# The last twelve chunks of a second expert weight in two column halves, eleven token tiles likewise

## The chip, the cores and the metric

The kernel runs on one core of a Trainium2 chip. Its time is the device time of one execution in microseconds (us); the program before has a median of 178.85 us over four runs (178.42 to 179.23). Engines are named as in the profile: PE is the matrix engine (PEld its weight load), DVE the vector engine, ACT the scalar engine, POOL is GpSimd, SP the sync engine. POOL and SP issue DMAs here: all loads of q, k, v and the expert weights go from POOL's queue (q0, with a cast from float32 to bfloat16 on the way), the stores of the result from SP's queue (q1).

## The reference, cut to what matters

Attention with a sliding window (heads 0 to 3) or a dilated one (heads 4 to 7), and behind it a soft mixture of 8 experts with 4 slots each.

```python
scores = q @ k.T / sqrt(64); masked to rel in [0, 32) or to every 4th of [0, 128)
x = softmax(scores) @ v              # 8 x 8 heads x 576 x 64 -> 4608 tokens x 512
logits = x @ phi                     # 4608 x 32 slots
d = exp(logits), normalised over the tokens;  slot_input = d.T @ x      # 32 x 512
for e in range(8):
    slot_out[e] = relu(slot_input[e] @ w1[e]) @ w2[e]     # 512 -> 1024 -> 512, 4 slots
c = exp(logits), normalised over the slots
out = c @ slot_out                   # 4608 x 512, float32
```

The result is 9.44 MB. The two weights, w1 and w2, are 16.8 MB each in float32.

## The kernel before

**Attention.** Eight units (a pair of batches and four heads each) are transposed, multiplied, masked and normalised. This part runs to about 131 us, and nothing in it is changed. It leaves `expT`, the exponentials of the logits by slot and token, and sums for the slot inputs.

**Experts.** w1 is held in seven parts of `WD` and one of `stg`. The hidden layer is in `hT` (16 chunks of 128 rows, slots as columns) at 141.5 us. The second layer accumulates in one pair of PSUM banks, `sp_`: column half 0 (output columns 0 to 255) in the first bank, half 1 in the second. w2 comes in groups of two experts; each partition holds 16 rows ("chunks" c of 512 columns, 32 KB of contiguous float32 in memory). The list `PARTS` (L893) gives the order in which PE consumes them (L901): p3a (group 3, chunks 0 to 7), p0, p1, p2, p3b (chunks 8 to 13) and p3c (chunks 14 and 15). `wload` (L444) loads each with one DMA, except p0, which goes out in 13 pieces (`skewed`, L460): 112 rows in four DMAs, 16 rows in small groups, and small reads into `scr` between them[...]. Six more tiny reads (`steps`, L815) go out between p2 and p3b.

**Output.** A row sum (`rsum`, L928) gives each token's normaliser, `rtok`. When the second layer is complete, DVE (L939) and ACT (L943) copy the two halves of `sp_` to `so_sb`. The 36 groups of 128 tokens are put into six token tiles of 1, 2, 3, 5, 9 and 16 groups (`TILES`, L887); the kernel calls a group j of such a tile. PE multiplies a group with `so_sb` (L973, 512 columns; the first group in two halves, L971), ACT and DVE by turns scale it into a staging area in SBUF (L985, L986), and when a tile is complete SP stores it with one DMA (L994). In memory a tile of n groups is n x 2 KB contiguous per partition.

**Order.** Every operation is entered with `op`, with a key and an assumed cost. `schedule` plays the program through with these costs and writes down, per engine, the order of the instructions; among operations that could start within 0.1 us of each other the smaller key goes first. POOL and SP keep the order in which their operations are entered. The semaphores follow from the data. A few plain matmuls with no use for the result are put in so that PE does not idle: a number in the stretches that the plan leaves empty (L1003), and seven (`WARM`) of them behind p2 (L917, key 1003.9, ahead of p3b with 1004).

Of the kernel before, what the change touches and what calls it, by code (L numbers as in the profile page):

```python
# [317 lines left out]
def bass_dilated_sliding_attn__then__soft_moe_slots_kernel(  # L318
# [14 lines left out]
    def sb(name, shape, dt=BF16):  # L333
# [3 lines left out]
    TURNS = ((15, None, 0), (6, 39, 8), (2, None, 0), (2, 7, 8), (6, None, 0), (6, 87, 8), (2, None, 0),  # L337
             (2, 23, 8), (7, None, 0))
    STEPS = (3, 2, 11, 4, 2, 10)
# [28 lines left out]
    scr = sb("scr", [16, len(TURNS), 2, 32])  # L368
# [25 lines left out]
    def bank(t):  # L394
        return ps[:, t.phys[0], :]
# [48 lines left out]
    def wload(name):  # L444
# [3 lines left out]
        if name[:2] == "w1":  # L448
            src = moe_w1[int(name[2:])].rearrange("(p c) f -> p c f", c=4)
            dst = ap.rearrange("p (c f) -> p c f", c=4)  # L450
        else:
            g = int(name[1])
            c = {"": slice(0, 16), "a": slice(0, 8), "b": slice(8, 14), "c": slice(14, 16)}[name[2:]]
            src = moe_w2[2 * g:2 * g + 2].rearrange("e (p c) f -> (e p) c f", c=16)[:, c, :]
            dst = ap.rearrange("p (c f) -> p c f", f=512)
        if name == "p0":
# [3 lines left out]
            def skewed(g):  # L460
                res = [g.dma_start(dst[r:128:n], src[r:128:n])
                       for r, n in ((0, 4), (1, 4), (2, 4), (3, 8))]
                for i, (n, r, step) in enumerate(TURNS):
                    if r is None:
                        res.append(g.dma_start(scr[0:n, i], src[0:n, :, 0:32]))
                    else:
                        e = r + step * (n - 1) + 1
                        res.append(g.dma_start(dst[r:e:step], src[r:e:step]))
                return res
            op("pool", skewed, after=b.prev, a=[b], cost=0.6 * (4 + len(TURNS)), sem=sem, nbytes=512 * 8192,  # L470
               nd=288, nq=4 + len(TURNS))
            return
        cut = [slice(None)]
        op("pool", lambda g: [g.dma_start(dst[:, x], src[:, x]) for x in cut], after=b.prev, a=[b],
           cost=0.6 * len(cut), sem=sem, nbytes=512 * ap.shape[1], nd=128 * len(cut), nq=len(cut))
# [4 lines left out]
    home(stg[:, 2, 4096:8192], [b_stg[2]], "p3a")  # L480
# [4 lines left out]
    home(TTf[:, 8192:11264], b_TT, "p3b")  # L485
    home(TTf[:, 11264:12288], b_TT, "p3c")
# [326 lines left out]
    s_scr = DmaSem(nc, "s_scr")  # L813

    def steps(g):  # L815
        res, lo = [], 8704
        for i, n in enumerate(STEPS):
            w = 8 * (i + 1)
            res.append(g.dma_start(stg[0:n, 0, lo:lo + w], moe_w1[0, 0:n, 0:w]))  # L819
            lo += w  # L820
        return res
    op("pool", steps, after=HOME["p0"][1].prev, cost=0.6 * len(STEPS), sem=s_scr, nbytes=16384,
       nd=8 * len(STEPS), nq=len(STEPS))
    wload("p3b")
    wload("p3c")
# [61 lines left out]
    for n in (1, 2, 3, 5, 9, 16):  # L887
        TILES.append((128 * sum(x[1] for x in TILES), n))
# [4 lines left out]
    PARTS = [("p3a", 3, 0, 8), ("p0", 0, 0, 16), ("p1", 1, 0, 16), ("p2", 2, 0, 16),  # L893
             ("p3b", 3, 8, 14), ("p3c", 3, 14, 16)]
    for k_, (name, g, c0, c1) in enumerate(PARTS):
        wv = HOME[name][0].rearrange("p (c f) -> p c f", f=512)
        for h_ in range(2):
            def pe(t, k_=k_, name=name, g=g, c0=c0, c1=c1, h_=h_, wv=wv):
                for c in range(c0, c1):
# [3 lines left out]
                                  wv[:, c - c0 + (1 if name == "p0" and c > 7 else 0), 256 * h_:256 * h_ + 256],  # L903
                                  start=(k_ == 0 and c < c0 + 4), stop=(k_ > 3 and c >= 12))
# [4 lines left out]
                       key=K1 + 2 + 0.5 * k_ + 0.1 * h_)  # L909
# [26 lines left out]
    for h_ in range(2):  # L936
        sl = slice(256 * h_, 256 * h_ + 256)
        if h_ == 0:
            op("dve", lambda vv, sl=sl: vv.tensor_scalar(so_sb[:, sl], pair(sp_)[:, 0, 0:256],  # L939
                                                         rcs[:, 0:1], None, op0=AluOp.mult),  # L940
               r=[b_sp[0], b_rcs], w=[b_so[0]], cost=0.35, key=K1 + 20)
        else:
            op("act", lambda ac, sl=sl: ac.activation(so_sb[:, sl], pair(sp_)[:, 1, 0:256],  # L943
                                                      ACTF.Copy, scale=rcs[:, 0:1]),
               r=[b_sp[1], b_rcs], w=[b_so[1]], cost=0.4, key=K1 + 20)

    for o_ in P.ops[-2:]:
# [4 lines left out]
    w17f, p0f = [HOME[x][0].bitcast(F32) for x in ("w17", "p0")]  # L952
    wdh = [f"w1{e}" for e in range(7)]
    STAGE = [(w17f[:, 0:512], ["w17"]), (w17f[:, 512:1536], ["w17"]),
             (WDf[:, 12800:14336], wdh), (p0f[:, 0:2560], ["p0"]),
             (WDf[:, 8192:12800], wdh), (WDf[:, 0:8192], wdh)]
    nev = 0
    for o, (t0, n) in enumerate(TILES):
        ost = STAGE[o][0].rearrange("p (j f) -> p j f", j=n)
        ob = Buf()  # L960
        for h_ in STAGE[o][1]:
            ob.prev = ob.prev + HOME[h_][1].ready + HOME[h_][1].reads
        for j0 in range(0, n, 2):
            po = tile(psum, 2)
            split = n == 1
            kk = K1 + 30 + o + 0.1 * j0
            b_po = [Buf(), Buf()]
            for j in range(2 if split else min(2, n - j0)):
                def pe(t, o=o, po=po, j0=j0, j=j, split=split):
                    if split:  # L970
                        return t.matmul(pair(po)[:, j, 0:256], tok[o][0],  # L971
                                        so_sb[:, 256 * j:256 * j + 256], start=True, stop=True)
                    return t.matmul(pair(po)[:, j, :], tok[o][j0 + j], so_sb[:],  # L973
                                    start=True, stop=True)
                p0 = op("pe", pe, r=(b_so[j:j + 1] if split else b_so) + b_expT, a=[po],
                        w=[b_po[j]], alloc=[po] if j == 0 else [], after=[p0] if j else [],
                        cost=0.12 if split else 0.22, key=kk + 0.01 * j)
                col = rcol[o] + (0 if split else j0 + j)

                def ev(en, po=po, ost=ost, j=j, j0=j0, split=split, col=col):  # L980
                    d_ = ost[:, 0, 256 * j:256 * j + 256] if split else ost[:, j0 + j, :]
                    s_ = pair(po)[:, j, 0:256 if split else 512]
                    sc_ = rtok[:, col:col + 1]
                    if en is nc.scalar:
                        return en.activation(d_, s_, ACTF.Copy, scale=sc_)  # L985
                    return en.tensor_scalar(d_, s_, sc_, None, op0=AluOp.mult)  # L986
                o_ = op(("dve", "act")[(j + nev) % 2], ev, r=[b_po[j], b_rtok], a=[ob], after=ob.prev,
                        cost=0.35 if split else 0.6, key=kk)
                o_.touch.append(po)
                po.left += 1  # L990
            nev += 0 if split else n - j0 == 1
        so = DmaSem(nc, f"s_out{o}")
        s_out.append(so)
        op("sp", lambda e, t0=t0, n=n, ost=ost: [e.dma_start(  # L994
# [62 lines left out]
```

## Time and profile before

| what | value |
|---|---|
| median of four runs | 178.85 us |
| the profiled execution's own time | 178.61 us |
| its span, first to last instruction | 176.9 us |
| granted TensorE clock, mean | 0.93 |
| busy: PE, DVE, ACT, POOL | 134.5, 113.0, 96.1, 44.1 us |
| read from memory, written to it | 61.94 MB, 9.44 MB |
| q0 (loads with cast), q1 (stores) | 30.95 MB and 9.50 MB moved |

The bytes of q0 are counted where they land, in bfloat16; twice as many are read. An engine's busy time is a sum over stages with different limits; the row of digits "DMA" on the profile's page shows in which tenth of each of 40 slices (4.4 us each) the 16 DMA engines were busy, and "PEclk" which clock PE was granted. In answers by stretch of time, "DMA share" can lie above 1.00, because the records of two packets on one DMA engine overlap a little.

### The profile page before, as it was taken

Reading aid. Unit: us, or ns where it says so; the run is one execution under the profiler, and the core shown is the slowest. Engines: PE = TensorE matmul, PEld = TensorE weight load, DVE = VectorE, ACT = ScalarE, POOL = GpSimd, SP = SyncE. Lnnn points to the kernel's source line nnn. Section 1 sums busy time; section 2 is a strip of 40 time slices with the busy share of each in tenths; the row PEclk is TensorE's granted clock in tenths of the full one; section 3 lists DMA queues with packets and bytes.
Section 4 is the critical chain, followed back from the end, with each engine's and each line's share of the span. In section 5 each row is a group of like instructions: output and inputs, shape, how many; then the busy total and the mean of one; then the engine's idle time right before and its main releaser. Section 6 shows DMA issues by size and latency. Waiting matters only on the chain.

```text
span 176.9 us, 5795 instructions
## 1 busy us (share of the span) xinstructions
PE 134.5 (76%) x2604; PEld 104.7 (59%) x2609; DVE 113.0 (64%) x256; ACT 96.1 (54%) x141; POOL 44.1 (25%) x87
## 2 busy tenths in 40 slices
PE   0019799779999896899968899986999997798000
PEld 0019698667897685697757778864656693342000
DVE  6850297936987995987974799899440200699300
ACT  2005779645985883977864788786311000699000
POOL 7990705202502501700200780107200000000000
PEclk9999999956999999999996999999999999789755
DMA  5999999999999999999999999999999998299995
GB/s 82 200 221 212 208 221 214 214 213 215 220 208 212 217 214 208 220 220 210 214 218 216 209 213 220 219 209 210 214 233 226 193 203 169 110 424 452 437 474 237
DMA packets 6504, 40.81 MB, mean 231 GB/s; under 512 B 2256, under 2 KB 2256, under 8 KB 2896
## 3 DMA queue, kind: packets, MB, share of 16 engines
q0 software_dynamic: 5088, 30.95, 84.7%
q1 hardware_dynamic: 1392, 9.50, 12.9%
q8 instruction: 20, 0.33, 0.7%
q14 instruction: 4, 0.03, 0.0%
HBM read 61.94 MB, written 9.44 MB: 404 GB/s over the span
## 4 chain that ended last, share of the span: by engine, by line
PE 45%; DMA 20%; DVE 11%; ACT 8%; issue 5%; POOL 3%; DVEq 0%; POOLq 0%
DMA TT<-in_moe_w_dram 15%; PE ps L576 11%; PE ps L571 7%; PE ps L668 5%; PE ps L614 5%; PE ps L639 5%; DMA stg<-in_k_dram 5%; DVE WD L986 4%; ACT PT L621 4%; PE ps L723 4%; PE ps L696 3%; ACT TT L596 3%; PE ps L973 2%; PE ps L754 2%; POOL stg L819 2%
## 5 line engine op out<-in xcount | busy, mean ns | idle before, releaser
L621 ACT ACTIVATE PT<-ps 128x768 bf16<-128x768 f32 x48 | 37.1, 816 | 10.5 <-PE ps L614 10.2
L596 ACT ACTIVATE TT<-ps 128x864 f32<-128x864 f32 x32 | 28.6, 896 | 21.7 <-PE ps L576 18.8
L679 DVE TENSOR_TENSOR XB<-ps,RV 96x768 bf16<-96x768 f32 x32 | 30.4, 951 | 0.9
L576 PE MATMUL ps<-ident,stg 96*64 96x96 bf16 x576 | 19.9, 241 | 14.5 <-DMA stg<-in_k_dram 12.5
L576 PEld LDWEIGHTS ps<-ident,stg 96*64 96x64 bf16 x576 | 17.8, 136 | 15.8 <-DMA stg<-in_k_dram 12.5
L644 DVE COPY VN<-ps 128x768 bf16<-128x768 bf16 x32 | 17.0, 542 | 11.5 <-PE ps L639 11.5
L614 PE MATMUL ps<-TT 64*128 64x96 bf16 x384 | 16.6, 214 | 7.3 <-issue 4.3
L668 PE MATMUL ps<-VN,PT 128*128 128x65 bf16 x384 | 18.5, 198 | 1.8 <-DVE XB L679 0.6
L428 POOL DMA_DIRECT2D stg<-in_q_dram x16 | 8.8, 551 | 43.1 <-PE ps L576 26.6
L668 PEld LDWEIGHTS ps<-VN,PT 128*128 128x128 bf16 x384 | 15.3, 101 | 3.2 <-DVE VN L644 0.9
L614 PEld LDWEIGHTS ps<-TT 64*128 64x128 bf16 x384 | 10.4, 99 | 11.4 <-issue 4.6
L639 PE MATMUL ps<-ident,TT 128*128 128x128 bf16 x192 | 16.1, 226 | 0.4 <-ACT PT L621 0.3
L709 ACT ACTIVATE XT<-ps 128x576 bf16<-128x576 bf16 x22 | 13.7, 652 | 2.6 <-PE ps L696 2.6
L571 PE MATMUL ps<-ident,stg 96*128 96x96 bf16 x288 | 14.7, 206 | 0.0
L696 PE MATMUL ps<-ident,XB 96*128 96x96 bf16 x192 | 13.2, 213 | 1.6 <-DVE XB L679 1.1
L629 DVE TENSOR_TENSOR PT<-PT,mask_p 128x768 bf16<-128x768 bf16 x24 | 12.8, 548 | 1.7 <-ACT PT L621 1.3
L571 PEld LDWEIGHTS ps<-ident,stg 96*128 96x128 bf16 x288 | 13.2, 98 | 1.0 <-issue 0.2
L629 DVE TENSOR_TENSOR PT<-PT,mask_d 128x768 bf16<-128x768 bf16 x24 | 13.0, 546 | 0.8 <-ACT PT L621 0.5
L639 PEld LDWEIGHTS ps<-ident,TT 128*128 128x128 bf16 x192 | 11.5, 100 | 2.3 <-ACT PT L621 0.5
L696 PEld LDWEIGHTS ps<-ident,XB 96*128 96x128 bf16 x192 | 9.9, 102 | 3.4 <-DVE XB L679 1.6
L973 PE MATMUL ps<-so_sb,expT 128*128 128x512 bf16 x34 | 10.8, 449 | 0.3 <-issue 0.2
L708 DVE COPY XT<-ps 128x576 bf16<-128x576 bf16 x10 | 5.8, 576 | 7.3 <-PE ps L696 7.1
(87 smaller groups left out, 183.5 us busy)
## 6 DMA issues: line engine op xcount, KB each, us to landing
WD<-in_moe_w_dram POOLq DMA_DIRECT2D x7, 1024.0 KB, 29.4
stg<-in_q_dram POOLq DMA_DIRECT2D x16, 288.0 KB, 19.4
stg<-in_v_dram POOLq DMA_DIRECT2D x16, 288.0 KB, 20.1
stg<-in_k_dram POOLq DMA_DIRECT2D x16, 288.0 KB, 21.0
out_dram<-WD SPq DMA_DIRECT2D x1, 4096.0 KB, 11.4
out_dram<-WD SPq DMA_DIRECT2D x1, 2304.0 KB, 7.0
stg<-in_moe_w_dram POOLq DMA_DIRECT2D x2, 1024.0 KB, 29.8
stg<-in_moe_w_dram POOLq DMA_DIRECT2D x1, 2048.0 KB, 24.2
```

What stands on the lines that cost most here:

```text
L571: i_ = t.transpose(bankb2(pt, a)[:, 96 * kk:96 * kk + 96], two[:, j // 2, c, :], ident[0:96, 0:96])
L576: i_ = t.transpose(bankb2(pt, a)[64 * hx:64 * hx + 64, 96 * kk:96 * kk + 96], src[:, hx, c, :], ident[0:96, 0:96])
L596: return ac.activation(d, sv, ACTF.Copy)
L614: i_ = t.matmul(pair(sc)[:, hx, QB * x:QB * x + QB], win(u, 1, h01, blk_, bpar)[64 * hx:64 * hx + 64], win(u, 0, h01, blk_, bpar)[64 * hx: ...
L621: op("act", lambda ac: ac.activation(sbt(pt)[:, 0:768].rearrange("p (x n) -> p x n", x=2), pair(sc)[:, :, 0:384], ACTF.Exp, scale=SCALE), ...
L629: return dv.tensor_tensor(p_, p_, m.unsqueeze(1).to_broadcast([128, 2, 384]), AluOp.mult)
L639: i_ = t.transpose(bankb(pv)[:, 128 * m:128 * m + 128], win(u, 2, h01, m, bpar), ident[:, :])
L644: op("dve", lambda dv: dv.tensor_copy(sbt(vn)[:, :, :, 0:64], bankb(pv)[:, 0:768].rearrange("p (m x d) -> p m x d", m=6, x=2)), r=[pv], w= ...
L668: i_ = t.matmul(pair(po)[:, bk, 65 * po_:65 * po_ + 65], sbt(pts[i])[:, o_:o_ + 128], sbt(vn)[:, m, half, 0:65], start=True, stop=True)
L679: op("dve", lambda dv: dv.tensor_tensor(sbt(xb)[:].rearrange("p m (x h d) -> p h x m d", x=2, h=2)[:, h01], pv()[:, :, :, 0:64], sbt(rv)[: ...
L696: i_ = t.transpose(bankb(px)[:, QB * m:QB * m + QB], sbt(xb)[:, m, 128 * x:128 * x + 128], ident[0:QB, 0:QB])
L973: return t.matmul(pair(po)[:, j, :], tok[o][j0 + j], so_sb[:], start=True, stop=True)
```

## The change

The last group of w2 is cut anew. p3a shrinks from eight chunks to four. The other twelve are loaded in two column halves: p3b and p3c hold chunks 4 to 13 and 14 to 15 for output columns 0 to 255, p3d and p3e the same chunks for columns 256 to 511. A run of such a load is 1 KB of float32 in memory and 512 bytes in SBUF. The four are entered behind p2 in this order, p3b now into a free part of `stg`. PE's work on p3d and p3e has a key 28 higher, behind the first token tiles of half 0.

The token tiles become 1, 2, 3, 5, 4, 8 and 13 groups. The first four (eleven groups) are computed and stored twice, first columns 0 to 255, then columns 256 to 511; the other three as before. In a halved tile two groups share a PSUM bank, and DVE empties such a bank with one `tensor_tensor` (the normaliser broadcast over 256 columns), ACT with two activations; the plan chooses between the two engines. A halved tile's store has runs of 1 KB in memory. There are 11 stores in place of six, all from SP's queue (`POOLS` is False). The tiles' staging areas move.

The second half of `so_sb` may be copied by DVE or ACT. The six tiny reads between p2 and p3b are removed, and p0's 13 pieces come in another order, with other small groups for its last 16 rows.

```diff
@@ -334,9 +334,11 @@
         return A(nc.sbuf_tensor(name, shape, dt))
 
     WARM = 7
-    TURNS = ((15, None, 0), (6, 39, 8), (2, None, 0), (2, 7, 8), (6, None, 0), (6, 87, 8), (2, None, 0),
-             (2, 23, 8), (7, None, 0))
-    STEPS = (3, 2, 11, 4, 2, 10)
+    TURNS = ((32, 0, 4), (32, 1, 4), (32, 2, 4), (16, 3, 8), (15, None, 0), (6, 39, 8), (2, None, 0),
+             (2, 87, 8), (6, None, 0), (4, 103, 8), (2, 7, 8), (2, None, 0), (2, 23, 8))
+    W2 = {"p3a": (3, 0, 4, 0, 512), "p0": (0, 0, 16, 0, 512), "p1": (1, 0, 16, 0, 512),
+          "p2": (2, 0, 16, 0, 512), "p3b": (3, 4, 14, 0, 256), "p3c": (3, 14, 16, 0, 256),
+          "p3d": (3, 4, 14, 256, 512), "p3e": (3, 14, 16, 256, 512)}
     NPT, NVN, NXB, NXT, NET = 6, 5, 5, 4, 2
     WD = sb("WD", [128, 7, 4096])
     stg = sb("stg", [128, 3, 9216])
...
@@ -449,41 +451,42 @@
             src = moe_w1[int(name[2:])].rearrange("(p c) f -> p c f", c=4)
             dst = ap.rearrange("p (c f) -> p c f", c=4)
         else:
-            g = int(name[1])
-            c = {"": slice(0, 16), "a": slice(0, 8), "b": slice(8, 14), "c": slice(14, 16)}[name[2:]]
-            src = moe_w2[2 * g:2 * g + 2].rearrange("e (p c) f -> (e p) c f", c=16)[:, c, :]
-            dst = ap.rearrange("p (c f) -> p c f", f=512)
+            g, c0, c1, f0, f1 = W2[name]
+            src = moe_w2[2 * g:2 * g + 2].rearrange("e (p c) f -> (e p) c f", c=16)[:, c0:c1, f0:f1]
+            dst = ap.rearrange("p (c f) -> p c f", f=f1 - f0)
         if name == "p0":
             src = src.rearrange("p (x c) f -> p x (c f)", x=2)
             dst = ap.rearrange("p (x y) -> p x y", x=2)[:, :, 0:4096]
 
             def skewed(g):
-                res = [g.dma_start(dst[r:128:n], src[r:128:n])
-                       for r, n in ((0, 4), (1, 4), (2, 4), (3, 8))]
+                res = []
                 for i, (n, r, step) in enumerate(TURNS):
                     if r is None:
-                        res.append(g.dma_start(scr[0:n, i], src[0:n, :, 0:32]))
+                        res.append(g.dma_start(scr[0:n, i], src[0:n, :, 0:8]))
                     else:
                         e = r + step * (n - 1) + 1
                         res.append(g.dma_start(dst[r:e:step], src[r:e:step]))
                 return res
-            op("pool", skewed, after=b.prev, a=[b], cost=0.6 * (4 + len(TURNS)), sem=sem, nbytes=512 * 8192,
-               nd=288, nq=4 + len(TURNS))
+            op("pool", skewed, after=b.prev, a=[b], cost=0.6 * (len(TURNS)), sem=sem, nbytes=512 * 8192,
+               nd=288, nq=len(TURNS))
             return
-        cut = [slice(None)]
-        op("pool", lambda g: [g.dma_start(dst[:, x], src[:, x]) for x in cut], after=b.prev, a=[b],
-           cost=0.6 * len(cut), sem=sem, nbytes=512 * ap.shape[1], nd=128 * len(cut), nq=len(cut))
+        op("pool", lambda g: [g.dma_start(dst, src)], after=b.prev, a=[b], cost=0.6, sem=sem,
+           nbytes=512 * ap.shape[1], nd=128)
 
     for e in range(7):
         home(WD[:, e, :], [], f"w1{e}")
     home(stg[:, 2, 0:4096], [b_stg[2]], "w17")
-    home(stg[:, 2, 4096:8192], [b_stg[2]], "p3a")
+    home(stg[:, 2, 4096:6144], [b_stg[2]], "p3a")
+    home(stg[:, 2, 6144:8704], [b_stg[2]], "p3b")
     home(stg[:, 0, :], [b_stg[0]], "p0")
     home(stg[:, 1, 0:8192], [b_stg[1]], "p1")
     TTf = TT[:].rearrange("p a x -> p (a x)")
     home(TTf[:, 0:8192], b_TT, "p2")
-    home(TTf[:, 8192:11264], b_TT, "p3b")
-    home(TTf[:, 11264:12288], b_TT, "p3c")
+    lo = 8192
+    for n_ in ("p3c", "p3d", "p3e"):
+        hi = lo + 256 * (W2[n_][2] - W2[n_][1])
+        home(TTf[:, lo:hi], b_TT, n_)
+        lo = hi
 
     load_unit(0)
     op("sp", lambda e: [e.dma_start(phi_st[:], moe_phi.rearrange("(c p) s -> p c s", p=128))],
@@ -810,19 +813,8 @@
             for bpar in range(2):
                 st_L(u - 1 + bpar, u)
     wload("p2")
-    s_scr = DmaSem(nc, "s_scr")
-
-    def steps(g):
-        res, lo = [], 8704
-        for i, n in enumerate(STEPS):
-            w = 8 * (i + 1)
-            res.append(g.dma_start(stg[0:n, 0, lo:lo + w], moe_w1[0, 0:n, 0:w]))
-            lo += w
-        return res
-    op("pool", steps, after=HOME["p0"][1].prev, cost=0.6 * len(STEPS), sem=s_scr, nbytes=16384,
-       nd=8 * len(STEPS), nq=len(STEPS))
-    wload("p3b")
-    wload("p3c")
+    for n_ in ("p3b", "p3c", "p3d", "p3e"):
+        wload(n_)
 
     K1 = 1000.0
     op("dve", lambda vv: vv.tensor_reduce(rcs[:], csum[:], mybir.AxisListType.X, AluOp.add),
@@ -884,29 +876,30 @@
         op("act" if p_ == 0 else "dve", ev, r=[ht], w=[b_hT[p_]], cost=0.35, key=K1)
 
     TILES = []
-    for n in (1, 2, 3, 5, 9, 16):
+    NSPLIT = 4
+    POOLS = False
+    for n in (1, 2, 3, 5, 4, 8, 13):
         TILES.append((128 * sum(x[1] for x in TILES), n))
     tok = [[expT[:, t0 + j:t0 + j + n * 127 + 1:n] for j in range(n)] for t0, n in TILES]
     rcol = [sum(n for _, n in TILES[:i]) for i in range(len(TILES))]
     sp_ = tile(psum, 2)
     b_sp = [Buf(), Buf()]
-    PARTS = [("p3a", 3, 0, 8), ("p0", 0, 0, 16), ("p1", 1, 0, 16), ("p2", 2, 0, 16),
-             ("p3b", 3, 8, 14), ("p3c", 3, 14, 16)]
-    for k_, (name, g, c0, c1) in enumerate(PARTS):
-        wv = HOME[name][0].rearrange("p (c f) -> p c f", f=512)
-        for h_ in range(2):
-            def pe(t, k_=k_, name=name, g=g, c0=c0, c1=c1, h_=h_, wv=wv):
+    for k_, name in enumerate(W2):
+        g, c0, c1, f0, f1 = W2[name]
+        wv = HOME[name][0].rearrange("p (c f) -> p c f", f=f1 - f0)
+        for h_ in range(f0 // 256, f1 // 256):
+            def pe(t, k_=k_, name=name, g=g, c0=c0, c1=c1, h_=h_, wv=wv, f0=f0):
                 for c in range(c0, c1):
                     j = c % 4
                     i_ = t.matmul(pair(sp_)[32 * j:32 * j + 32, h_, 0:256],
                                   hT[:, c, 24 * g:24 * g + 32],
-                                  wv[:, c - c0 + (1 if name == "p0" and c > 7 else 0), 256 * h_:256 * h_ + 256],
-                                  start=(k_ == 0 and c < c0 + 4), stop=(k_ > 3 and c >= 12))
+                                  wv[:, c - c0 + (name == "p0" and c > 7), 256 * h_ - f0:256 * h_ - f0 + 256],
+                                  start=(k_ == 0 and c < 4), stop=(k_ > 3 and c >= 12))
                 return i_
             last_ = op("pe", pe, r=b_hT + [HOME[name][1]], alloc=[sp_] if k_ == h_ == 0 else [],
                        a=[sp_, b_sp[h_]], cost=0.13 * (c1 - c0) / 4, mode="c",
                        ni=2 * (c1 - c0),
-                       key=K1 + 2 + 0.5 * k_ + 0.1 * h_)
+                       key=K1 + 2 + 0.5 * k_ + 0.1 * h_ + (28 if k_ > 5 else 0))
             if k_ == 2:
                 mid = last_
         if k_ == 3:
@@ -935,65 +928,83 @@
 
     for h_ in range(2):
         sl = slice(256 * h_, 256 * h_ + 256)
...
     for o_ in P.ops[-2:]:
         o_.touch.append(sp_)
         sp_.left += 1
 
...
     nev = 0
-    for o, (t0, n) in enumerate(TILES):
+    for o, h_ in [(o, h_) for h_ in range(2) for o in range(NSPLIT)] + [(o, None) for o in range(NSPLIT, 7)]:
+        t0, n = TILES[o]
         ost = STAGE[o][0].rearrange("p (j f) -> p j f", j=n)
+        sl = slice(0, 512) if h_ is None else slice(256 * h_, 256 * h_ + 256)
         ob = Buf()
-        for h_ in STAGE[o][1]:
-            ob.prev = ob.prev + HOME[h_][1].ready + HOME[h_][1].reads
+        for x in STAGE[o][1]:
+            ob.prev = ob.prev + HOME[x][1].ready + HOME[x][1].reads
+        k1 = K1 + 30 + o + 10 * (2 if h_ is None else h_)
+        w = sl.stop - sl.start
         for j0 in range(0, n, 2):
-            po = tile(psum, 2)
-            split = n == 1
-            kk = K1 + 30 + o + 0.1 * j0
+            po = tile(psum, w // 256)
+            kk = k1 + 0.1 * j0
             b_po = [Buf(), Buf()]
-            for j in range(2 if split else min(2, n - j0)):
-                def pe(t, o=o, po=po, j0=j0, j=j, split=split):
-                    if split:
-                        return t.matmul(pair(po)[:, j, 0:256], tok[o][0],
-                                        so_sb[:, 256 * j:256 * j + 256], start=True, stop=True)
-                    return t.matmul(pair(po)[:, j, :], tok[o][j0 + j], so_sb[:],
-                                    start=True, stop=True)
-                p0 = op("pe", pe, r=(b_so[j:j + 1] if split else b_so) + b_expT, a=[po],
+
+            def slot(j, po=po, w=w):
+                if w == 512:
+                    return pair(po)[:, j, :]
+                return bank(po)[:, w * j:w * j + w]
+            m = min(2, n - j0)
+            for js in [range(m)] if w == 256 else [(j,) for j in range(m)]:
+                def pe(t, o=o, slot=slot, j0=j0, js=js, sl=sl):
+                    for j in js:
+                        i_ = t.matmul(slot(j), tok[o][j0 + j], so_sb[:, sl], start=True, stop=True,
+                                      skip_group_check=True)
+                    return i_
+                j = js[0]
+                p0 = op("pe", pe, r=(b_so if h_ is None else b_so[h_:h_ + 1]) + b_expT, a=[po],
                         w=[b_po[j]], alloc=[po] if j == 0 else [], after=[p0] if j else [],
-                        cost=0.12 if split else 0.22, key=kk + 0.01 * j)
-                col = rcol[o] + (0 if split else j0 + j)
-
-                def ev(en, po=po, ost=ost, j=j, j0=j0, split=split, col=col):
-                    d_ = ost[:, 0, 256 * j:256 * j + 256] if split else ost[:, j0 + j, :]
-                    s_ = pair(po)[:, j, 0:256 if split else 512]
-                    sc_ = rtok[:, col:col + 1]
-                    if en is nc.scalar:
-                        return en.activation(d_, s_, ACTF.Copy, scale=sc_)
-                    return en.tensor_scalar(d_, s_, sc_, None, op0=AluOp.mult)
-                o_ = op(("dve", "act")[(j + nev) % 2], ev, r=[b_po[j], b_rtok], a=[ob], after=ob.prev,
-                        cost=0.35 if split else 0.6, key=kk)
+                        cost=0.22 if h_ is None else 0.15 * m, key=kk + 0.01 * j, ni=2 * len(js))
+                col = rcol[o] + j0 + j
+
+                def ev(en, slot=slot, ost=ost, js=js, j0=j0, sl=sl, col=col, po=po):
+                    if en is nc.vector and len(js) == 2:
+                        return en.tensor_tensor(
+                            ost[:, j0:j0 + 2, sl], bank(po).rearrange("p (j f) -> p j f", j=2),
+                            rtok[:, col:col + 2].unsqueeze(2).to_broadcast([128, 2, 256]), AluOp.mult)
+                    for j in js:
+                        d_, s_, sc_ = ost[:, j0 + j, sl], slot(j), rtok[:, col + j - js[0]:col + j - js[0] + 1]
+                        if en is nc.scalar:
+                            i_ = en.activation(d_, s_, ACTF.Copy, scale=sc_)
+                        else:
+                            i_ = en.tensor_scalar(d_, s_, sc_, None, op0=AluOp.mult)
+                    return i_
+                if w == 256:
+                    o_ = op(("dve", "act"), ev, r=[b_po[j], b_rtok], a=[ob], after=ob.prev,
+                            cost={"dve": 0.7 if m == 2 else 0.48, "act": 0.47 * m}, key=kk)
+                else:
+                    o_ = op(("dve", "act")[nev % 2], ev, r=[b_po[j], b_rtok], a=[ob], after=ob.prev,
+                            cost=0.66, key=kk)
+                    nev += 1
                 o_.touch.append(po)
                 po.left += 1
-            nev += 0 if split else n - j0 == 1
-        so = DmaSem(nc, f"s_out{o}")
+        so = DmaSem(nc, f"s_out{o}_{h_}")
         s_out.append(so)
-        op("sp", lambda e, t0=t0, n=n, ost=ost: [e.dma_start(
-            out[t0:t0 + 128 * n, :].rearrange("(p j) f -> p j f", j=n), ost)],
-            r=[ob], cost=0.1, sem=so, nbytes=262144 * n, key=K1 + 30 + o)
+        op("pool" if POOLS and h_ is not None and (h_ or o > 1) else "sp",
+           lambda e, t0=t0, n=n, ost=ost, sl=sl: [e.dma_start(
+               out[t0:t0 + 128 * n, sl].rearrange("(p j) f -> p j f", j=n), ost[:, :, sl])],
+           r=[ob], cost=0.1, sem=so, nbytes=512 * n * w, key=k1)
 
     def filler(n):
         t = tile(psum, 1)
```

## The prediction

> **What bounds the kernel now.** I read first the page's rows of 40 slices, for what is busy all the way.
>
> ```profile
> DMA  5999999999999999999999999999999998299995
> GB/s 82 200 221 212 208 221 214 214 213 215 220 208 212 217 214 208 220 220 210 214 218 216 209 213 220 219 209 210 214 233 226 193 203 169 110 424 452 437 474 237
> ```
>
> The DMA engines are full from the second slice on, but for two digits: 8 and 2, slices 33 and 34 (146 to 155 us). Before them loads run at some 215 GB/s (counted in bfloat16), behind them stores at some 430. PE's 76% and DVE's 64% are no bound; only idle DMA time can be won, or DMA work added. Next the answer by stretches of time around that hole:
>
> ```profile
> core 0: us, PE busy (x) PEld busy (x) DVE busy (x) ACT busy (x) POOL busy (x), PEclk, DMA share, GB/s
> 127.00:143.00 16.00, 15.74 (x220) 9.93 (x224) 3.76 (x10) 1.72 (x4) 0.00 (x0) 1.00 1.04 223
> 149.00:151.00 2.00, 0.79 (x16) 0.44 (x16) 0.00 (x0) 0.00 (x0) 0.00 (x0) 1.00 0.26 46
> 151.00:153.40 2.40, 1.93 (x11) 0.84 (x8) 1.87 (x4) 1.64 (x3) 0.00 (x0) 0.76 0.00 0
> 154.30:157.60 3.30, 3.30 (x14) 1.57 (x11) 3.10 (x5) 3.00 (x5) 0.00 (x0) 0.79 1.03 417
> 158.00:160.00 2.00, 1.77 (x6) 0.70 (x8) 2.00 (x4) 2.00 (x5) 0.00 (x0) 1.00 1.03 430
> 166.50:174.80 8.30, 0.00 (x0) 0.00 (x0) 0.00 (x0) 0.00 (x0) 0.00 (x0) 0.50 1.00 430
> ```
>
> Share 0.26 of 2 us: the average engine stops loading at 149.0 + 0.52 = 149.5 us. The trace's records of single packets, which no view prints, add: last load packet's end 150.46, first store packet 153.47, last 176.07. So the average engine is idle for 4.0 us. The timeline shows what fills them:
>
> ```profile
> 141.69 2.37 PE L901 MATMUL ps<-stg,hT 128*32 128x256 bf16 x80
> 143.99 2.04 PE L928 MATMUL ps<-rowm,expT 128*128 128x1 bf16 x36
> 145.96 1.06 PE L901 MATMUL ps<-TT,hT 128*32 128x256 bf16 x32
> 147.18 1.46 PE L917 MATMUL ps<-mask_p,ident 128*128 128x512 bf16 x6 [0.16 <-issue]
> 149.56 0.61 PE L901 MATMUL ps<-TT,hT 128*32 128x256 bf16 x12 [0.93 <-DMA TT<-in_moe_w_dram]
> 150.82 0.40 PE L901 MATMUL ps<-TT,hT 128*32 128x256 bf16 x4 [0.65 <-DMA TT<-in_moe_w_dram]
> 151.15 0.48 DVE L939 TENSOR_SCALAR so_sb<-ps,rcs 128x256 bf16<-128x256 f32 x1 [4.70 <-PE ps L901]
> 151.69 0.39 PE L971 MATMUL ps<-so_sb,expT 128*128 128x256 bf16 x2 [0.47 <-DVE so_sb L939]
> 152.02 1.14 DVE L986 TENSOR_SCALAR stg<-ps,rtok 128x256 f32<-128x256 f32 x2 [0.38 <-PE ps L971]
> 152.63 0.35 SPq L994 DMA_DIRECT2D out_dram<-stg  x1
> ```
>
> From p3c's first matmul (150.82, 0.36 behind its last packet) it takes 2.65 us to the first store packet: 0.33 to the copy, 0.54 to the first token matmul, 0.33 to its eviction, 0.61 to SP's issue, 0.84 to the packet.
>
> **The price of a packet.** All bytes stay; their runs get shorter. In the packet records, starts on one engine follow at 154, 455, 606 and 1,208 ns for loaded packets of 2,048, 6,144, 8,192 and 16,384 bytes: 3.4 ns + 0.0735 ns per byte. Stores of 2,048, 4,096, 10,240 and 32,768 bytes follow at 84.5, 159, 387 and 1,213 ns: 9 ns + 0.0368 per byte. The records themselves last longer for loads (173 ns at 2,048 bytes, 1,229 at 16,384: 22 ns fixed), but overlap; so the share reads 1.04.
>
> **Loads.** p3b to p3e have 128 x 24 = 3,072 runs of 512 bytes where 1,536 KB went in 384 runs of 4,096 (from p3a), 6,144 and 2,048 bytes per partition, p3a being cut in half. Taken as 8 packets per engine and DMA: before 24 packets, after 8 (p3a) + 192. So 176 more at 3.4 ns: +0.60 us; average end 150.1, slowest 151.06. An outer half (p3b or p3d, 80 packets of 41.0 ns) is 3.28 us and p3c or p3e (16) 0.66, so half 0 is in 3.94 us before the end: 147.1 on the slowest engine.
>
> **POOL.** Six DMAs of `steps` go (six of 510 ns: 3.1 us), two of about 0.55 come; p0's 13 stay 13. All wait behind up to 25 us of queued loads (p3c: issued at 124.4, landed at 150.8), so this is worth 0. That queue also covers the writing of 1,280 descriptors where 128 cost 0.55 us: between no growth (2 to 11 rows cost 0.51 already) and tenfold, 5.5 us each, p3e would be issued by about 134, needed at 149. I take 0. How the 16 loose rows of p0 fall on the engines moves the slowest end against the average (now 0.96 apart) by perhaps half a microsecond either way; I take 0, since the next step hides it.
>
> **PE decides the first store.** p3a gives 8 matmuls in place of 16, so L901's 80 become 72: 2.07 us. p2 now lands some 2.4 us earlier, but the row sum keeps its place: 141.69 + 2.07 + 2.0 (row sum) + 1.0 (p2) + 1.7 (the seven `WARM` matmuls, 146.94 to 148.64 before) = 148.4. p3b's ten matmuls add 0.29, so p3c's first one starts at 148.7, although its data is usable at 147.1 + 0.36 = 147.5. First store packet: 148.7 + 2.65 = 151.35, in place of 153.47: 2.12 earlier. Behind `WARM` wait p3b, p3c, the copy, then every store; that is the new hold.
>
> **Evictions.** One `tensor_tensor` empties two halves on DVE: nearest row L679, 951 ns for 768 columns with a broadcast; at 1.04 ns a column for the difference, 0.68 for 512. ACT takes 2 x 0.475 (its L985 on 256 columns). Together some 5 halves per us, 640 GB/s or more: above the stores' 430. The first tiles are ready at 0, 0.6, 1.05 and 1.95 us behind the first; against store times of 0.37 and 0.75 that leaves 0.23 us of DMA idle. For the tile of 13, PE, DVE and ACT at 0.35 us per group (25 groups in 8.64 us at L986) are done by 163.8, its packets possible at 164.8; the DMA gets there at 167.
>
> **Half 1.** p3e's last packet at 151.06 gives first stores at 154.1; with its copy behind half 0's evictions (to 152.3) at 154.7. Half 0's stores last to 155.7. So this wait is hidden, by 1.0 us.
>
> **Stores.** Before: 8 packets per engine of each size, (84.5 + 159 + 237 + 387 + 687 + 1,213) x 8 = 22.14 us; elapsed 22.60. After: 2,816 runs of 1 KB, 176 per engine at 46.6 ns = 8.20, and (310 + 611 + 987) x 8 = 15.27: 23.47, so +1.33.
>
> Here the Trainium skill is weighed. "DMA: Bandwidth & Descriptors", Specifications, puts the minimum for line rate at 512 bytes; by it short runs cost nothing. "Advanced Engine Details and Errata", Clock Domains, gives 42 to 43 ns for a 1 KiB descriptor. At 42.5 the 176 cost 7.48: +0.6 us. The rows' straight line says 46.6 and no smaller store is in the trace; I take the line.
>
> Against the change speaks the first page's Measured section: a batch should be 1 MiB or more, and a DMA costs about 2 us plus its bytes at 436 GB/s. Eight stores here are 128 to 640 KB; five more DMAs in a row would be +10 us. The row from 154.3 to 157.6 contradicts that for queued stores: three stores of 512 to 1,280 KB overlap there at a share of 1.03. So 0 for the count.
>
> **Sum.** 151.35 + 0.23 + 23.47 = 175.05 for the last packet, against 176.07: -1.0 us. Against the profiled execution's own 178.61: 177.6. That execution is 0.24 below the median of 178.85; against the median it is 177.8, my forecast. A measurement of this kernel can tell about 0.5% (0.9 us) from no change.
>
> **Rivals.** *A, cheaper runs or an earlier start (0.22).* Runs at the skill's price (-0.7), and PE early enough that the data alone holds the first store (150.2 instead of 151.35): -1.7 to -2.7, so 176.2 to 177.2. For: the hole is 4.0 us, 1.1 of it still open in my sum. Against: `WARM` has the smaller key.
>
> *B, slow short loads (0.20).* Slower than before. Place: p3b to p3e on the load queue. If a 512-byte run occupies its engine for the 60 ns of a record (22 fixed) and not for 41, 176 x 22 = 3.9 us come on top of the old end: average 153.4, slowest 154.3. Half 0 then is data-bound (148.6 + 0.36 + 2.65 = 151.6), shares the engines with 1.8 us of loads, p3e ends at about 155.9, half 1's stores start at 158.9 and the end is 158.9 + 4.1 + 15.3 = 178.3: +2.2, 181.1 on the median. It decides from about 14 ns per packet on, where added loads eat the 1.0 us. For: no load in the trace has runs over 128 and under 2,048 bytes. Against: the spacing of 154 ns, and pairs of 64-byte packets 7 ns apart.
>
> *C, the order (0.08).* If the plan puts p3d ahead of half 0's token matmuls, these wait for p3d (151.06 - 0.66 + 0.36 = 150.8), the first store for 152.9: +0.5, 179.3. Against: p3d's key is 1033.1, half 0's are 1030 to 1033.4, and p3d lands late.
>
> My forecast has 0.50. Of it 0.28 lies beyond 0.9 us, as A does: faster 0.50. The remaining 0.22, and 0.05 of C, are within: same 0.27. B and the rest of C: slower 0.23. The range leaves out the lower end of A and the upper half of B: 176.1 to 180.3.
>
> **What would show it.** First SP issue near 150.5 (now 152.63); a `WARM` row ending near 148.4 with p3b's matmuls next and no DMA wait before them; a store stream without holes from 152 on; last packet near 175. Wrong, if p3b's matmuls wait for DMA, if the stretch of p3b to p3e moves clearly under 200 GB/s, if stores of 1 KB runs fall under 340 GB/s, or if SP's fifth issue waits for the second half's copy.

## The result and the profile after

The changed kernel takes 0.9948 of the time before, with a 95% interval of 0.9931 to 0.9964: 0.9 us of 178.7 less. The ratio leaves out, as possibly slowed by the chip, runs more than 1.5% above their kernel's fastest: ten of the 43 of the changed kernel and its profiled one (180.6 us), but none of the 64 before. The medians of all runs are 178.31 us (176.86 to 182.14) and 178.67 us before (178.19 to 180.19): 0.36 us apart. The account below makes late runs the kernel's own in part, and to that extent the gain is nearer to 0.36 us than to 0.9. The single runs spread over more than 5 us where they spread over 2 before. What spreads them is the main finding below.

I read the changed kernel's profiles from two later runs: experiment e8, span 175.4 us (177.12 us), and experiment e0, span 178.1 us (179.81 us). First the slices of e8, granted clock and DMA:

```profile
PEclk9999999978999999999995799999999999969655
DMA  5999999999999999999999999999999999999996
GB/s 78 206 210 218 210 214 210 219 212 216 217 212 218 214 214 215 217 212 212 218 212 213 219 213 214 218 213 227 204 224 228 198 185 198 266 342 429 470 401 291
```

The hole of two digits is gone in e8's DMA row: 9 up to the last slice. (In e0, where the first store comes later, one digit of 5 stays.) In exchange the bytes per slice sink: 185 and 198 GB/s in slices 32 and 33 (140 to 149 us), where the short loads run, and 342 in slice 35, where short stores run. (Slices count from 0.) The same by stretches of time, e8 again:

```profile
core 0: us, PE busy (x) PEld busy (x) DVE busy (x) ACT busy (x) POOL busy (x), PEclk, DMA share, GB/s
142.50:149.00 6.50, 5.19 (x79) 3.51 (x79) 1.21 (x3) 0.13 (x1) 0.00 (x0) 1.00 1.44 196
149.50:151.00 1.50, 0.44 (x11) 0.22 (x10) 1.27 (x3) 1.31 (x4) 0.00 (x0) 1.00 0.85 159
151.50:159.00 7.50, 6.60 (x30) 3.71 (x31) 6.56 (x11) 5.60 (x11) 0.00 (x0) 0.77 1.02 344
160.00:162.00 2.00, 1.68 (x6) 0.53 (x5) 2.00 (x4) 2.00 (x5) 0.00 (x0) 1.00 1.04 430
```

The share of 1.44 in the first row is no overload: records of 60 ns follow each other every 42 ns on an engine and are counted twice where they overlap. The measure is the 196 GB/s beside it. Now the timeline around the first store, e8, where PE was in time (SPq is SP's queue of DMA issues):

```profile
139.79 2.15 PE L894 MATMUL ps<-stg,hT 128*32 128x256 bf16 x72
144.93 1.46 PE L910 MATMUL ps<-mask_p,ident 128*128 128x512 bf16 x6 [0.16 <-issue]
146.82 0.51 PE L894 MATMUL ps<-stg,hT 128*32 128x256 bf16 x10 [0.43 <-DMA stg<-in_moe_w_dram]
147.46 0.29 PE L894 MATMUL ps<-TT,hT 128*32 128x256 bf16 x2
149.16 2.53 SPq L1005 DMA_DIRECT2D out_dram<-stg  x4
150.77 0.51 PE L894 MATMUL ps<-TT,hT 128*32 128x256 bf16 x10 [1.06 <-DMA TT<-in_moe_w_dram]
```

and e0, the same program, where PE came 3.6 us later out of the work before:

```profile
143.35 2.15 PE L894 MATMUL ps<-stg,hT 128*32 128x256 bf16 x72
148.26 1.69 PE L910 MATMUL ps<-mask_p,ident 128*128 128x512 bf16 x7
149.88 0.51 PE L894 MATMUL ps<-stg,hT 128*32 128x256 bf16 x10
150.11 0.28 PE L894 MATMUL ps<-TT,hT 128*32 128x256 bf16 x2
151.84 1.85 SPq L1005 DMA_DIRECT2D out_dram<-stg  x3
```

L910 are the seven plain matmuls, L894 behind them p3b (ten) and p3c (two). In e8 they end early and p3b waits for its data; in e0 p3b follows without a wait. The packet records give the first store packets, 150.01 and 152.68, and the end of the last ones, 174.59 and 177.28. Between them lie 24.58 and 24.60 us; before it was 22.60. So the change lengthens the store stream by 1.98 us, and pays as soon as the first store comes more than 1.98 us before 153.47, that is before 151.5. (The four halved tiles hold eleven groups of 128 tokens; the "eleven token tiles" of the title are these groups.)

### The profile page after: what moved, and what is told of

The parts are those of the page before. It is cut to its first block, busy times and chain, and to the rows that moved or that the text cites. A ratio compares the mean times of both kernels' runs of the same rounds, so it can differ in the third digit from the quotient of the medians.

```text
span 178.9 us, 5823 instructions
## 1 busy us (share of the span) xinstructions
PE 134.5 (75%) x2614; PEld 106.6 (60%) x2619; DVE 113.5 (63%) x259; ACT 95.8 (54%) x144; POOL 43.6 (24%) x83
## 4 chain that ended last, share of the span: by engine, by line
PE 51%; DVE 23%; issue 6%; ACT 5%; DMA 5%; POOL 1%; DVEq 0%; POOLq 0%
PE ps L579 9%; PE ps L574 6%; PE ps L726 5%; DMA stg<-in_k_dram 5%; DVE PT L632 5%; PE ps L671 5%; PE ps L642 4%; PE ps L617 4%; DVE XB L682 4%; DVE VN L647 4%; DVE WD L991 4%; PE ps L699 4%; PE ps L1014 3%; ACT TT L599 2%; PE ps L757 2%
## 5 line engine op out<-in xcount | busy, mean ns | idle before, releaser
L624 ACT ACTIVATE PT<-ps 128x768 bf16<-128x768 f32 x48 | 37.1, 815 | 11.4 <-PE ps L617 10.9
L579 PE MATMUL ps<-ident,stg 96*64 96x96 bf16 x576 | 19.3, 235 | 14.5 <-DMA stg<-in_k_dram 12.6
L579 PEld LDWEIGHTS ps<-ident,stg 96*64 96x64 bf16 x576 | 17.2, 132 | 15.9 <-DMA stg<-in_k_dram 12.6
L671 PE MATMUL ps<-VN,PT 128*128 128x65 bf16 x384 | 19.0, 200 | 3.2 <-issue 2.0
L642 PE MATMUL ps<-ident,TT 128*128 128x128 bf16 x192 | 17.5, 237 | 0.7 <-ACT PT L624 0.3
L642 PEld LDWEIGHTS ps<-ident,TT 128*128 128x128 bf16 x192 | 12.4, 105 | 2.9 <-DVE VN L647 0.6
L699 PEld LDWEIGHTS ps<-ident,XB 96*128 96x128 bf16 x192 | 10.5, 106 | 2.3 <-DVE XB L682 1.2
L972 PE MATMUL ps<-so_sb,expT 128*128 128x512 bf16 (+1 forms) x46 | 9.4, 333 | 2.6 <-DVE so_sb L935 1.7
L989 ACT ACTIVATE stg<-ps,rtok 128x256 f32<-128x256 f32 (+1 forms) x12 | 5.1, 512 | 10.4 <-PE ps L972 10.4
```

Source lines behind the costliest of these rows:

```text
L579: i_ = t.transpose(bankb2(pt, a)[64 * hx:64 * hx + 64, 96 * kk:96 * kk + 96], src[:, hx, c, :], ident[0:96, 0:96])
L624: op("act", lambda ac: ac.activation(sbt(pt)[:, 0:768].rearrange("p (x n) -> p x n", x=2), pair(sc)[:, :, 0:384], ACTF.Exp, scale=SCALE), ...
L642: i_ = t.transpose(bankb(pv)[:, 128 * m:128 * m + 128], win(u, 2, h01, m, bpar), ident[:, :])
L671: i_ = t.matmul(pair(po)[:, bk, 65 * po_:65 * po_ + 65], sbt(pts[i])[:, o_:o_ + 128], sbt(vn)[:, m, half, 0:65], start=True, stop=True)
L699: i_ = t.transpose(bankb(px)[:, QB * m:QB * m + QB], sbt(xb)[:, m, 128 * x:128 * x + 128], ident[0:QB, 0:QB])
```

## The experiments

All ratios are to the kernel before on the same chip: e0 to e3 ran on one chip, e4 to e7 on a second, e8 to e11 on a third.

**e0, e8: the changed kernel again.**

> The changed kernel itself, for a second profile and for its spread. Theory 'PE holds the first store': PE reaches the last matmuls of the first column half at the time its earlier work lets it, with no wait for DMA before them, so a PE that comes later from the attention moves the end one for one; ratio to before 0.995, single runs spread over 2 us or more, first store packet between 150.5 and 153.5 us and last packet 23.5 to 24.7 us behind it. Rival 'the loads hold it': p3b's matmuls wait for DMA, and the spread is that of the kernel before (1 us).

> The changed kernel again, as the measure for the next three on the same chip: ratio 0.994 to 0.998, spread 2 us or more, its fastest runs near 177.0 us, where the loads and not PE hold the first store.

e0: 0.9966 (0.9928 to 1.0003), runs from 177.2 to 180.8. e8: 0.9936 (0.9900 to 0.9973), 176.9 to 180.7. In e8 six of twelve runs lie at 176.9 to 177.3 and six at 179.0 to 180.7; nothing between. The two profiles show the theory's form in one and the rival's in the other: with PE in time the loads hold the first store, with PE late PE does, and the end follows. In all nine profiles of kernels with four halved tiles (first stores from 150.0 to 155.3 us) the stream lasts 24.56 to 24.60 us, but for one at 24.99: in e2 the second store's packets start 1.4 us behind the first ones, in the others 1.0 to 1.1. Why is open.

**e1: the row sum ahead of the fold.** The fold is the group of matmuls that adds up the parts of the slot inputs, ahead of the hidden layer. One op of 36 matmuls becomes four of nine, free to be planned earlier:

```diff
...
-    op("pe", rsum, r=b_expT + [b_rowm], w=[rs], alloc=[rs], cost=2.0, key=K1 + 3, ni=72,
-       after=[mid])
...
+    for x in range(4):
+        ...
+        op("pe", rsum, r=b_expT + [b_rowm], alloc=[rs] if x == 0 else [], cost=0.5, key=K1 + 0.9,
+           ni=18, **{"w" if x == 0 else "a": [rs]})
```

> Changed kernel, but the row sum (36 matmuls, 2.0 us between the first three w2 groups and p2) is cut in four and put where PE fills gaps at 128 to 132 us. Theory 'PE holds the first store': the first half's matmuls start 1 to 2 us earlier until their data holds them (a DMA wait before p3b or p3c appears), first store packet near 150.2, ratio to before 0.985 to 0.989 (176.0 to 176.7 us), and single runs spread less. Rival 'the loads hold it' or 'the short runs' price is all': same time as the changed kernel, 0.995.

0.9948 (0.9915 to 0.9982), runs from 177.1 to 183.1: no gain over the changed kernel in the ratio (the theory's 0.985 to 0.989 fell), and a wider spread. The profiled run is one of the late ones (182.19 us, first store at 155.09, not near 150.2). Its clock row and the stretch of the hidden layer:

```profile
PEclk9999999997599997599997899999995899999755
...
134.80:141.50 6.70, 6.70 (x53) 3.46 (x56) 0.68 (x2) 0.19 (x1) 0.00 (x0) 0.50 0.96 205
```

PE ran at half clock through the fold and the first hidden product. The row sum's matmuls of one column had taken the place of plain 512-column ones just ahead of them. This run was late before that too: its last exponential of the attention starts at 122.74 us, 4.6 behind e8's.

**e5: the row sum in the gaps of the hidden layer, without the seven plain matmuls.** Three parts of 8, 14 and 14 matmuls, tied behind the fold, the first product and the transposes:

```diff
-    WARM = 7
+    WARM = 0
...
+    for x, (n_, g_) in enumerate(((8, g_fo), (14, ffn1), (14, g_ht))):
+        ...
+        op("pe", rsum, r=b_expT + [b_rowm], alloc=[rs] if x == 0 else [], cost=0.055 * n_, key=K1 + 0.9,
+           ni=2 * n_, after=[g_], **{"w" if x == 0 else "a": [rs]})
```

> Changed kernel without the seven plain matmuls behind p2, and with the row sum's 36 matmuls put in three parts into the gaps behind the fold, the first hidden product and the hidden transposes, where plain matmuls stood. PE then reaches p3b some 3.7 us earlier than in the changed kernel. Theory 'PE holds the first store until the data does': first store at 149.8 to 150.4 us in every run, ratio 0.989 to 0.992, single runs within 1 us, because a PE late by 2 us is still in time. Rival 'another bound lies close behind': no better than leaving out the seven matmuls alone (0.992); rival 'clock': above 0.995.

0.9963 (0.9928 to 0.9997); five runs at 177.0 to 177.2, seven from 178.3 to 180.6. The expectation fell: some 3.7 us less work ahead of p3b narrowed nothing. The clock row and timeline of a late run (179.61 us, first store at 152.53):

```profile
PEclk9999999998799999699996999999997857999655
...
142.48 1.00 PE L922 MATMUL ps<-rowm,expT 128*128 128x1 bf16 x14
143.42 4.03 PE L894 MATMUL ps<-stg,hT 128*32 128x256 bf16 x72
147.38 1.46 PE L1015 MATMUL ps<-mask_p,ident 128*128 128x512 bf16 x3
148.77 1.11 PE L894 MATMUL ps<-TT,hT 128*32 128x256 bf16 x32
149.72 0.49 PE L894 MATMUL ps<-stg,hT 128*32 128x256 bf16 x10
```

The same 72 matmuls take 4.03 us here and 2.15 in e0 and e8; three plain ones 1.46 (0.82 elsewhere). In this run half clock took back what the moved row sum won. Both kernels with the row sum in place of plain matmuls were at half clock somewhere between 130 and 145 us, and of the fourteen profiles no other was. That is one profile of each, both of late runs, so the link is suggested and not shown; from 146 us on e4, e7 and e11 fall to half clock as well, with the row sum in its old place. Until the work ends, half-clock stretches in these traces last 3.4 us, 6.8 or once 10.2 (e11), multiples of one length. The length fits the Trainium skill ("TensorE: Matmul & The Clock Gate", Part 1), by which the clock is set from how busy PE was in windows of about 3.4 us that do not start with the kernel. Which matmuls count as busy the traces do not show: in e1's row PE's records fill all 6.70 us, and it stayed at half clock for two windows.

**e2, e9: without the seven plain matmuls**, all else as changed (`WARM = 0`).

> Changed kernel without the seven plain matmuls behind p2 (1.7 us on PE, no use for the result). Theory 'PE holds the first store': 1.0 to 1.7 us earlier first store, ratio 0.986 to 0.990. Rival 'PE's clock': without them PE idles, its granted clock falls in the stretch of the token matmuls, and the evictions behind slow matmuls give the gain back: 0.994 to 0.998.

> Changed kernel without the seven plain matmuls, once more. If PE lateness is what spreads the runs, 1.5 us less on PE ahead of the first store narrows the spread and gives 0.990 to 0.995 again; if the narrow spread of the first time was the chip's, it is as wide as the changed kernel's.

e2: 0.9924 (0.9900 to 0.9949), between theory and rival, all runs within 177.3 to 178.2. e9, on another chip beside e8: 0.9947 (0.9918 to 0.9976), 177.1 to 180.6. e2 gains 0.4% over e0 and e9 loses 0.1% to e8, both within the intervals, and the narrow spread of the first did not come back. In e9's profile PE starts the 72 matmuls at 144.79, 5 us later than in e8: 1.7 us less work cannot make up for that. Inconclusive for the time; no version here beats the changed kernel beyond doubt.

**e6, e7: fourteen plain matmuls instead of seven**, in the changed kernel and in the one before (`WARM = 14`).

> Changed kernel with fourteen plain matmuls behind p2 instead of seven: PE is 1.5 us later at p3b, everything else equal. Theory 'PE holds the first store': the end moves by nearly all of it, ratio 1.002 to 1.005. Rival 'the loads hold it': 0.995 as the changed kernel.

> Kernel before with the same fourteen plain matmuls. Theory 'before, the loads hold the first store': PE waits 0.9 and 0.65 us for p3b and p3c there, which takes up nearly all of the 1.5 us; ratio 1.000 to 1.003. If PE held it there too: 1.007 to 1.009.

e6: 1.0025 (0.9992 to 1.0059). Against e0 and e8 (0.9966, 0.9936) that is 0.6 to 0.9%, or 1.1 to 1.6 us for 1.5 us of added PE work, with some 0.6 us of uncertainty in each ratio. e7: 1.0025 (1.0005 to 1.0045), 0.45 us (0.1 to 0.8). Both as the theory had it: PE's delay goes into the end of the changed kernel nearly whole, and into the one before by about a third. e7's runs fall into two groups, four at 178.4 to 178.8 and eight at 179.5 to 179.9 us; a run of the second group:

```profile
145.91 1.90 PE L901 MATMUL ps<-TT,hT 128*32 128x256 bf16 x32 [1.24 <-DMA TT<-in_moe_w_dram]
147.75 3.93 PE L917 MATMUL ps<-mask_p,ident 128*128 128x512 bf16 x14
151.61 0.62 PE L901 MATMUL ps<-TT,hT 128*32 128x256 bf16 x16
```

The fourteen fell into a half-clock stretch, took 3.93 us instead of the 3.20 of e6, and p3b and p3c then ran without waiting. The first store of this run is at 154.62, 1.15 us behind the one before.

**e3: the halved loads alone** (`NSPLIT = 0`, no tile halved).

> The halved loads alone: all seven token tiles with 512 columns, so no store before both halves are complete. Theory (a short run costs 3 to 4 ns more on a load): first store at the place of before or 0.6 us behind it, stores of the old length, ratio 1.003 to 1.005 (179.2 to 179.6 us). Rival 'slow short loads' (22 ns a run): ratio 1.02. If the halved loads were worth something without halved stores: under 1.000.

1.0049 (1.0026 to 1.0071), +0.9 us: the theory's upper end. The rival's 1.02 is out. In its profile the loads end 0.6 us later than before (151.06 against 150.46), as foreseen, but the first store is at 154.64, 1.17 later; PE was at half clock there from 151.2 us on. The stream lasts 22.87 us.

**e4: the halved stores alone**, with w2 cut as before:

```diff
-    W2 = {"p3a": (3, 0, 4, 0, 512), "p0": (0, 0, 16, 0, 512), "p1": (1, 0, 16, 0, 512),
-          "p2": (2, 0, 16, 0, 512), "p3b": (3, 4, 14, 0, 256), "p3c": (3, 14, 16, 0, 256),
-          "p3d": (3, 4, 14, 256, 512), "p3e": (3, 14, 16, 256, 512)}
+    W2 = {"p3a": (3, 0, 8, 0, 512), "p0": (0, 0, 16, 0, 512), "p1": (1, 0, 16, 0, 512),
+          "p2": (2, 0, 16, 0, 512), "p3b": (3, 8, 14, 0, 512), "p3c": (3, 14, 16, 0, 512)}
...
```

> The halved stores alone: w2's last group loaded as before the change (p3a of eight chunks, p3b and p3c in full width), token tiles and stores as changed. Both halves are then complete together, so nothing starts early. Theory (a 1 KB run of a store occupies its engine 47 ns where 75 are paid for 2 KB or more in longer runs): first store where it was before, 1.3 to 1.6 us more for the stores, ratio 1.007 to 1.010 (180.0 to 180.6 us). Rival 'runs from 512 bytes on cost nothing': 1.000 to 1.002.

1.0095 (1.0076 to 1.0114), +1.7 us. Its first store packet is at 153.49, that of before at 153.47, and its stream lasts 24.59 us: the price of the stores by itself. e4 also keeps the new order of p0's pieces and has no tiny reads, so in this profile these two did not move the first store. Each half of the change loses. If the prices of e3 and e4 add, paying both without an early start would cost 2.6 us, so the early start is worth some 3.5 us where the sum gains 0.9.

**e10, e11: three and two tiles halved** (`NSPLIT = 3` and `2`, both with `WARM = 0`).

> Without the seven matmuls, three token tiles halved instead of four (six groups, the tile of five whole). Each group that is not halved saves 8 packets a engine of some 20 ns, 0.16 us, so 0.8 us; but the first half's stores then last 2.3 us instead of 4.2, and the second half's first packet comes some 4.1 us behind the first store where the loads hold both. Theory 'cover': the saving goes into a hole before the second half, same time as with four halved within 0.3 us. Rival 'price of runs alone': 0.8 us faster.

> As before it, two token tiles halved (three groups). Saved 1.3 us of short runs, stores of the first half last 1.1 us: a hole of 1.9 to 2.5 us before the second half. Theory 'cover': 0.6 to 1.2 us slower than with four halved. Rival 'price of runs alone': 1.3 us faster.

e10: 0.9984 (0.9962 to 1.0007), 0.7 us over e9. e11: 1.0016 (0.9997 to 1.0036), 1.2 us over e9. "The price of runs alone", which foresaw 0.8 and 1.3 us less, is out. "Cover" is right for e11; for e10 the loss is larger than the 0.3 us that it allowed. The hole, in e10 and then in e11:

```profile
core 0: us, PE busy (x) PEld busy (x) DVE busy (x) ACT busy (x) POOL busy (x), PEclk, DMA share, GB/s
151.00:153.20 2.20, 1.29 (x16) 0.88 (x17) 0.83 (x2) 0.00 (x0) 0.00 (x0) 0.71 0.92 311
153.20:155.40 2.20, 1.98 (x8) 0.91 (x7) 1.73 (x4) 1.83 (x4) 0.00 (x0) 0.51 0.19 66
...
150.30:152.30 2.00, 1.14 (x12) 0.40 (x12) 0.31 (x1) 0.00 (x0) 0.00 (x0) 0.50 0.68 209
152.30:155.50 3.20, 2.75 (x8) 1.31 (x10) 2.16 (x4) 1.94 (x4) 0.00 (x0) 0.50 0.13 43
```

The first half's stores are out, the second half's are not there: 2.2 us at a share of 0.19, 3.2 us at 0.13. With four tiles the row from 151.5 to 159.0 of e8 stood at 1.02. The streams last 26.09 and 26.65 us in place of 24.58. PE is at half clock in both holes, but that is not what made them: the second half's first packets come 4.19 and 4.05 us behind the first store, and 4.1 was foreseen from the loads alone. What was not foreseen is a second gap: in e10 the next small store then starts 1.13 us behind, where its predecessor takes 0.38. In e8 no such gap stands there (0.37).

## Why the prediction was right, and where its terms were off

Forecast: 1.0 us less on the profiled execution's own time, 177.8 us against the median. Measured: 0.52% of 178.7, 0.9 us (0.36 by the medians of all runs). The number was right in part by luck. Two terms were off in opposite directions, and the forecast is one number for a time that moves by almost 4 us from run to run: of e8's twelve runs none lies between 177.4 and 178.9.

- **The hole is what can be won, and added DMA work is what it costs.** Held, by e3, e4 and e8's DMA row.
- **A packet costs its spacing, not its record.** Held for loads: 42.1 ns measured for 512 bytes, 41.0 foreseen, records of 60. Rival B, built on the records, would have been 2% in e3.
- **p3c usable at 147.5 on the slowest engine.** Held: e8's PE starts it at 147.46.
- **PE decides the first store, at 151.35.** The mechanism held in e0, where PE ran the seven matmuls and then p3b without a DMA wait (first store at 152.68), and by e6. The number did not: I took one profile's PE chain (141.69 for the 72 matmuls) as fixed. It starts at 139.79 in e8, 143.35 in e0 and 144.79 in e9. In e8, one of the fastest runs, the second half of rival A is there instead: the data alone hold the first store, at 150.01 (150.2 in A), and p3b waits 0.43 us for DMA, which the prediction had named as a sign of being wrong. A's cheaper runs did not come.
- **The store stream, 23.47 + 0.23 = 23.70 us.** The term that was mis-sized: 24.58, 0.9 us more. About half of that could be seen beforehand: the same prices give 22.14 us for the stream before, which took 22.60, and the 0.46 was not carried over. In the new stream a 1 KB run takes 47.6 to 48.1 ns and not 46.6, which is 0.2 us over 176 of them. The first small stores leave more idle than 0.23: the second one's packets start 1.0 us behind the first one's (0.6 foreseen), and e0's row below has a share of 0.49 over 1.40 us, 0.7 us idle. The other 0.2 lies in the long tiles and at the end.

```profile
152.60:154.00 1.40, 0.33 (x11) 0.11 (x2) 1.24 (x3) 0.88 (x3) 0.00 (x0) 1.00 0.49 165
```

- **The Trainium skill's prices.** The 512 bytes for line rate ("DMA: Bandwidth & Descriptors", Specifications) would leave the stores at 22.1 us, and the 42 to 43 ns ("Advanced Engine Details and Errata", Clock Domains) at 22.8; the stream took 24.6. The straight line through the trace's rows was nearest and still low. The 2 us per DMA, which the DMA page has not under Measured but in its section "Anatomy of one DMA — SWDGE (gpsimd) path", for DMAs from GpSimd, had no place in this queue of stores from SP: e8's row has 1.02 while seven of the eight halved stores run.
- **Half 1 hidden by 1.0 us.** Held with four halved tiles, by some 0.6 us: in e8 half 1's stores start at 154.86, right behind half 0's last, and in e10 and e11 they could start at 154.21 and 154.31. These two show the wait when the cover is shorter.
- **Rival C, the order.** It did not come: in e8 half 0's token matmuls start at 148.33, p3d's at 150.77.
- **POOL, at nothing.** Held. In e8 POOL issues p3b in 0.98 us and p3c to p3e in 2.38, and is done with them at 122.3 us (p3e's data land at 151.1):

```profile
118.45 0.56 POOL L473 DMA_DIRECT2D TT<-in_moe_w_dram  x1 [7.87 <-PE ps L617]
119.00 0.98 POOL L473 DMA_DIRECT2D stg<-in_moe_w_dram  x1
119.96 2.38 POOL L473 DMA_DIRECT2D TT<-in_moe_w_dram  x3
```

What is settled in part: why PE comes to the 72 matmuls up to 5 us earlier or later in executions of the same program. From the start of the attention's last exponential (ACT, L624) to these matmuls, in e8, e9 and e0 (the granted clock stands third from the end):

```profile
core 0: us, PE busy (x) PEld busy (x) DVE busy (x) ACT busy (x) POOL busy (x), PEclk, DMA share, GB/s
118.19:139.79 21.60, 19.70 (x239) 12.12 (x242) 9.32 (x23) 5.01 (x11) 3.90 (x5) 1.00 1.05 220
123.19:144.79 21.60, 19.70 (x239) 12.12 (x243) 9.31 (x23) 5.01 (x11) 3.90 (x5) 1.00 1.05 210
120.30:143.35 23.05, 21.44 (x242) 13.05 (x243) 9.31 (x23) 5.01 (x11) 3.90 (x5) 0.93 1.04 212
```

At full clock this stretch takes 21.5 or 21.6 us in every profile that has the row sum in its old place; in the four with one half-clock stretch of 3.4 us inside it (e0, e2, e3, e6) it takes 23.0, 1.4 us more. The rest of the lateness is there before the last exponential, which starts anywhere from 117.4 to 123.2 us. The three profiles with the most half clock before it (17 to 20 us: e1, e9 and the one recorded with the result) are the three latest, 122.6 to 123.2 us; the others have 7 to 14. That suggests the clock as the cause there too, but no run isolated it.

## What to carry to other kernels

When DMA is full but for one hole, weigh the hole against the longer stream that filling it needs: here 22.60 us of stores became 24.58, so the first store had to come 2 us earlier before anything was won. Price a short packet by the distance from start to start in the trace, not by its record, give the first small stores of a stream an idle time of their own, and carry over what the same prices miss in the stream that you can measure. And look at what the old wait was covering: before, PE had about 0.9 us to spare at that point, and when the loads no longer hold it, a delay of PE's work ahead can reach the end of the kernel nearly whole (e6).

## What the runs showed of the hardware that I had not expected

A half-clock stretch of 3.4 us cost 1.4 us of PE's time between the attention and the second layer (23.0 us in place of 21.6, four profiles), and in the changed kernel such a delay can reach the end. Matmuls with one column in the place of 512-column ones went with a halved PE clock in the profiles of both kernels that tried it (e1: 0.50 from 134.8 to 141.5 us; e5: 72 matmuls in 4.03 us instead of 2.15), so work moved into a gap that plain matmuls had filled was not free there. Stores with runs of 1 KB move 344 GB/s against 430 for long ones, and loads with runs of 512 bytes (1 KB read) 196 against 217 for packets of 16 KB (one every 1,208 ns on each of 16 engines).
